# Work lists of a fused convolution and expert kernel, refilled: fewer first singles, more second pairs, and one group's scatters without an index copy

## The chip, the cores and the metric

The kernel runs on one core of a Trainium2 chip. Its time is the device time of one execution in microseconds (us). Before the change the median of three runs is 1198.82 us (1196.96 to 1201.81). A difference of under 0.5% is not told from no change here.

## The reference, cut to what matters

The input `x` is 8 x 2880 x 192, so there are 23040 tokens of 192 numbers. First comes a causal convolution with its own weights at each token: 7 taps for each of 8 heads of 24 numbers, normalised by a softmax.

```
w = exp(weight_gen - max) / sum                 # per token and head, 7 taps
x[s, h, :] = sum_k w[s, h, k] * x_pad[s + k, h, :]
g = argmax(x @ w_group)                         # 4 groups
e = argmax(x @ w_expert[g])                     # 4 experts in the group
out = p_g * p_e * (relu(x @ w1[g, e]) @ w2[g, e])   # 192 -> 1024 -> 192
```

Each token goes to one of 16 experts. All is float32.

## The kernel before, in words

**Two halves that overlap.** The *front* makes tokens ready: convolution, scores, choice of the expert, and a scatter that sends each token's row to its place in a table `rows` in device memory. There each expert has its own stretch (two experts share one from both ends). The *blocks* read runs of rows of one expert from that table, do the two matrix products, and scatter the result to `out`. The 180 columns of 128 tokens are worked in 15 groups of 12 columns (`WIDTHS`). TensorE does the products; VectorE does nearly all of the convolution; ScalarE evacuates and casts; GpSimd issues the scatters; SyncE loads weights and rows.

**Lists.** After certain groups VectorE writes a *list*: which expert's rows the next blocks take. An entry of `ROUNDS` is (groups finished, triples, pairs, singles): a single is a block of 128 rows, a pair of 256, a triple of 384. So the first list, after two groups, has ten singles; the second, after the third group, has four pairs; and so on, 14 lists in all. Before the last list, a slot takes full units of 128 rows only. The last list also has `SHORT` = (7, 4) slots: seven blocks of 320 rows and four of 192, for experts whose last unit is at most half full. How many blocks there are, and of what kind, is fixed when the program is written; which expert each takes is read at run time (SyncE loads an offset and an expert number from the list, L816, L830). What does not fit falls to a tail of conditional blocks (`tail`, L1193).

**Three kinds of arithmetic.** A single is *plain*: full float32 products. Pairs and triples up to the twelfth list are *whole* (`whole`, L1023): w1 and x are split into high and low parts and the first product takes five faster passes, the second product is full float32. From the thirteenth list on (`WHOLE = 12`) w2 is split as well (L870 to L876), and the second product takes the passes of L993 and L994.

**Order of the work.** The order on TensorE, ScalarE, VectorE and SyncE is written out by hand when the program is built. `blocks` (L1035) goes through all blocks unit by unit: it emits the first product (`gemm1`, L940), the second with a lag of two units (`gemm2`, L974), the transposes of the next block (`prep_x`, L910: L926 and L927, for singles L915), and the loads. After every unit `fill` puts in steps of the front until a planned VectorE clock has come up to the planned TensorE clock plus a margin (`AHEAD`). So VectorE's front work is laid beside TensorE's blocks, step by step, by planned costs. A pair also takes VectorE time for the low parts of w1 and x (L861, L936, recorded at the helper's L883); a single takes none.

**From a group to its list.** `ranks` (L440) ends with each token's place (`posi`, L503), then GpSimd scatters 12 columns (L505 to L507), then `table` writes the list. A block's rows may be loaded (L818) only when the scatters of its list's last group have landed. For groups in `SPACED` each scatter first copies its column of row numbers to a ring of three small tiles (L514 to L516), and so a fourth scatter waits until the first has read its numbers; groups outside `SPACED` scatter straight from `posi`:

```
for s in range(n):
    run("pool", 2.2 if g in SPACED else 1.28, clk["dve"])
    scatter_row(pi[:, s:s + 1], xrow[s // SC][:, s % SC, :], round_of(g), g in SPACED)
```

The scatters of results (L1008) stand in the same GpSimd program. At most eight result tiles `y` are in use.

Of the kernel before, what the change touches and what calls it, by code (L numbers as in the profile page):

```python
# [17 lines left out]
DRAM = bass.MemoryType.DRAM  # L18

WIDTHS = (12,) * 15  # L20
ROUNDS = ((2, 0, 0, 10), (3, 0, 4, 0), (4, 0, 5, 0), (5, 0, 7, 0), (6, 0, 5, 0), (7, 0, 7, 0), (8, 0, 5, 0), (9, 0, 6, 0), (10, 0, 7, 0), (11, 0, 5, 0), (12, 1, 4, 0), (13, 0, 5, 0), (14, 0, 6, 0), (15, 3, 2, 2))
SHORT = (7, 4)
LATE = (1.0, 3.0, 3.0)
AHEAD = (1.0, 1.0, 2.5)
HURRY = 12
SPACED = range(2, 15)
HALVES = (36.0, 42.0, 48.0, 54.0, 60.0, 66.0, 72.0, 78.0)
WHOLE = 12
SINGLE = tuple((k,) for k in range(7))
# [13 lines left out]
def conv_moe_kernel(ctx: ExitStack, tc: tile.TileContext, x, wgen, w_group, w_expert, w1, w2, out):  # L43
# [26 lines left out]
    MAXB = NTOK // BK  # L70
    NR = len(ROUNDS)
    ENDS = [r[0] for r in ROUNDS]
    COL = [sum(WIDTHS[:g]) for g in range(len(WIDTHS) + 1)]
# [5 lines left out]
    FIRST = ENDS[0]  # L79
    MAIN = next(r[0] for r in ROUNDS if r[1] or r[2])  # L80
    kinds = ((3, 1), (2, 2), (1, 3))
# [4 lines left out]
    sure = 0  # L86
    for r in ROUNDS[:-1]:
        for nb, c in kinds:
            sure = max(sure, min(sure + nb * UB * r[c], COL[r[0]] * P - NE * (nb * UB - 1)))
    left = (NTOK - sure + NE * (BK - 1)) // BK  # L90
    TAIL = max(0, -(-(left - ROUNDS[-1][2]) // TB))

# [162 lines left out]
    def run(eng, cost, *deps):  # L255
        clk[eng] = max([clk[eng]] + [d + HOP for d in deps]) + cost
        return clk[eng]
# [10 lines left out]
    def round_of(g):  # L268
        return next(r for r in range(NR) if g < ENDS[r])
# [170 lines left out]
    def ranks(g, o, ls, tls):  # L440
# [64 lines left out]
# [3 lines that stand above are left out]
        if g + 1 in ENDS:  # L508
# [3 lines left out]
    def scatter_row(idx, src, r, spaced):  # L512
        ix = idx
        if spaced:  # L514
            ix = new_ix()
            nc.gpsimd.tensor_copy(out=ix, in_=idx)  # L516
        written_once(nc.gpsimd.indirect_dma_start(  # L517
            out=rows[:, :], out_offset=bass.IndirectOffsetOnAxis(ap=ix, axis=0),
            in_=src, in_offset=None, bounds_check=NROW - 1, oob_is_err=False), r)
# [11 lines left out]
    def table(r):  # L531
# [17 lines left out]
        if last:  # L549
# [5 lines left out]
            v.scalar_tensor_tensor(out=at, in0=units, scalar=-3.0, in1=done, op0=ALU.add, op1=ALU.add)  # L555
            for nb, odd, start, slots in ((4, half, at, SHORT[0]), (5, two, None, SHORT[1])):
                cums = yield from listing(r, nb, odd, t, False, start)
# [3 lines left out]
                yield 0.6  # L561
        todo = [(nb, c) for nb, c in ((kinds[0], kinds[2], kinds[1]) if last else kinds) if ROUNDS[r][c] or last and nb == 2]
        for nb, c in todo:
# [32 lines left out]
    def listing(r, nb, n, t, counted, at=None):  # L596
        v = nc.vector
        per = tiles_of(nb)
        at = done if at is None else at
        cume, cums, org = t("cume"), t("cums"), t("org")  # L600
        own, tv, ri = t("own"), t("tv"), t("ri", (P, 2))
        tab = tabs[r, nb] = tb.tile([P, 3], I32, name=f"tab{nb}", bufs=1 if nb in CUT else 4)
        q0 = qp[:, 0:1]
        v.tensor_tensor_scan(out=cume, data0=smask[SG][:, :, 1], data1=n, initial=0.0, op0=ALU.mult, op1=ALU.add)
        v.tensor_tensor(out=cums, in0=cume, in1=n, op=ALU.subtract)
        v.tensor_scalar(out=past[:, 1:], in0=cume, scalar1=q0, scalar2=None, op0=ALU.is_le)
        v.scalar_tensor_tensor(out=org, in0=cums, scalar=float(per), in1=at, op0=ALU.mult, op1=ALU.subtract)
        v.tensor_tensor(out=own, in0=past[:, 0:NE], in1=past[:, 1:], op=ALU.subtract)
        v.scalar_tensor_tensor(out=tv, in0=org, scalar=qb[:, per - 1:per], in1=down, op0=ALU.subtract, op1=ALU.mult)
        v.tensor_reduce(out=ri[:, 1:2], in_=past[:, 1:], axis=AX.X, op=ALU.add)  # L610
        yield 0.9
        v.tensor_tensor(out=tv, in0=tv, in1=first[nb], op=ALU.add)
        v.tensor_scalar(out=tab[:, 1:2], in0=ri[:, 1:2], scalar1=float(NE - 1), scalar2=None, op0=ALU.min)
        v.tensor_tensor(out=tv, in0=tv, in1=own, op=ALU.mult)
        if counted:
            v.tensor_copy(out=tab[:, 2:3], in_=cume[:, NE - 1:NE])
        v.tensor_reduce(out=ri[:, 0:1], in_=tv, axis=AX.X, op=ALU.add)
        v.tensor_scalar(out=tab[:, 0:1], in0=ri[:, 0:1], scalar1=float(NROW), scalar2=None, op0=ALU.add)
        yield 0.9
        return cums  # L620
# [163 lines left out]
    for r, spec in enumerate(ROUNDS):  # L784
        for nb, c in kinds:
            order += [(r, nb, q) for q in range(spec[c])]
            if r == NR - 1:
                order += [(r, k, q) for j, k in enumerate(CUT) if CUT[k] == nb for q in range(SHORT[j])]
    visits = {}
# [442 lines left out]
```

## Time and profile before

| | |
|---|---|
| runs, median (range) | 1198.82 us (1196.96 to 1201.81) |
| the profiled execution | 1198.2 us, span 1196.6 us, granted clock 0.987 |
| TensorE busy | 1125.1 us, 94% |
| VectorE busy | 955.8 us, 80% |
| ScalarE busy | 643.9 us, 54% |
| GpSimd busy | 583.6 us, 49% |
| moved | 275.10 MB, mean 230 GB/s |

A row of the profile names the line of the kernel, the engine (PE is TensorE, DVE VectorE, ACT ScalarE, POOL GpSimd), the operation, the tiles it writes and reads, and its count; in a group row the busy time, the mean duration in ns and the idle time before it follow. In a row of the timeline the start and the duration in us come first, and in brackets the idle time of the engine just before and what ended it.

### The profile page before, as it was taken

How to read it: one execution, taken by the hardware profiler on the slowest of the kernel's cores; microseconds unless marked ns; L12 is line 12 of the kernel's file. 1: busy time of each engine (PE TensorE's matmuls, PEld its weight loads, DVE VectorE, ACT ScalarE, POOL GpSimd, SP SyncE). 2: the span in 40 equal slices, each digit the busy share in tenths (PEclk: the TensorE clock that was granted, in tenths of full speed). 3: DMA queues.
4: the chain of work that ended last, by engine and by line, in shares of the span. 5: the costliest groups of instructions: out<-in, count | busy, mean ns of one | idle time of the engine just before them, and what ended most of it. 6: DMA issues, size and time to landing. Idle time of an engine off the chain costs nothing.

```text
span 1196.6 us, 24607 instructions
## 1 busy us (share of the span) xinstructions
PE 1125.1 (94%) x8357; PEld 1062.7 (89%) x8357; DVE 955.8 (80%) x1682; ACT 643.9 (54%) x1235; POOL 583.6 (49%) x613
## 2 busy tenths in 40 slices
PE   5887999999999999999999999999799899999998
PEld 2444888999999999999989999999699899999997
DVE  8899997989998989998988889898374576655661
ACT  1332435555555555565546556565446676555762
POOL 7164284647274745765564738384636312222211
PEclk9898999999999999999999999999999999999999
DMA  5797999887878877778786868767657875655562
GB/s 172 216 312 227 298 310 286 247 272 229 286 233 255 256 249 235 248 246 281 221 284 197 289 202 281 232 181 227 201 154 235 263 241 154 189 174 179 161 200 76
DMA packets 84521, 275.10 MB, mean 230 GB/s; under 512 B 15491, under 2 KB 34379, under 8 KB 82593
## 3 DMA queue, kind: packets, MB, share of 16 engines
q1 hardware_dynamic: 64056, 229.77, 61.3%
q0 software_dynamic: 20208, 43.39, 11.9%
q8 instruction: 67, 1.10, 0.4%
q14 instruction: 70, 0.57, 0.1%
q10 hardware_dynamic: 120, 0.28, 0.1%
HBM read 225.83 MB, written 48.42 MB: 229 GB/s over the span
## 4 chain that ended last, share of the span: by engine, by line
PE 62%; issue 19%; DVE 6%; POOL 4%; ACT 3%; DMA 3%; another core or an unknown queue 2%; POOLq 1%; SPq 0%; DVEq 0%; ACTq 0%
PE py L991 27%; PE ph L953 25%; POOL out L1008 4%; DVE pr L307 2%; PE pl L389 2%; PE ph L348 1%; PE tpx L927 1%; PE tpx L926 1%; DMA xb<-rows 1%; PE tpx L348 1%; PE tp L406 1%; DMA rows<-rem 1%; PE py L348 1%; PE pl L406 1%
## 5 line engine op out<-in xcount | busy, mean ns | idle before, releaser
L953 PE MATMUL ph<-xh,wa 128*128 128x256 f32 (+3 forms) x1992 | 455.5, 303 | 1.2 <-issue 1.1
L1008 POOL DMA_INDIRECT out<-y,xb x189 | 213.9, 1132 | 425.6 <-ACT y L1000 176.7
L991 PE MATMUL py<-wc,hh 128*128 128x192 f32 x2160 | 401.3, 327 | 2.7 <-ACT y L1000 2.2
L953 PE MATMUL ph<-xl,wa 128*128 128x256 f32 (+3 forms) x1328 | 351.9, 286 | 0.3
L991 PEld LDWEIGHTS py<-wc,hh 128*128 128x128 f32 x2160 | 346.0, 190 | 4.7 <-ACT y L1000 2.8
L953 PEld LDWEIGHTS ph<-xh,wa 128*128 128x128 f32 x1992 | 337.7, 190 | 4.2 <-issue 2.1
L959 ACT ACTIVATE hh<-ph 128x512 f32<-128x512 f32 (+2 forms) x296 | 165.9, 561 | 265.9 <-PE ph L953 239.0
L953 PEld LDWEIGHTS ph<-xl,wa 128*128 128x128 f32 x1328 | 252.1, 190 | 1.1 <-issue 0.8
L307 DVE TENSOR_TENSOR pr<-xin,wt 128x1152 f32<-128x1152 f32 x186 | 249.3, 1351 | 4.7 <-PE py L348 3.4
L517 POOL DMA_INDIRECT rows<-xrow,ix x156 | 222.2, 1424 | 45.6 <-POOL ix L516 31.5
L325 DVE TENSOR_TENSOR xrow<-xrow,pr 128x1152 f32<-128x1152 f32 x144 | 194.9, 1353 | 0.7
L883 DVE SCALAR_TENSOR_TENSOR pr<-ph,hh 128x320 fp32r<-128x320 f32 (+2 forms) x128 | 71.7, 560 | 92.5 <-ACT hh L964 85.6
L883 DVE TENSOR_TENSOR wa<-raw,wa 128x1024 fp32r<-128x1024 f32 x83 | 101.3, 1220 | 31.9 <-ACT wa L859 30.7
L516 POOL COPY ix<-posi 128x1 int32<-128x1 int32 x156 | 76.0, 499 | 79.1 <-DMA rows<-xrow,ix 44.7
L993 PE MATMUL py<-wc,hh 128*128 128x384 f32 x352 | 111.6, 364 | 0.0
L964 ACT ACTIVATE hh<-ph 128x320 fp32r<-128x320 f32 (+2 forms) x128 | 63.8, 499 | 72.0 <-PE ph L953 71.1
L994 PE MATMUL py<-wc,pr 128*128 128x192 f32 x352 | 88.5, 251 | 0.0
L859 ACT CAST wa<-raw 128x1024 fp32r<-128x1024 f32 x83 | 87.1, 1050 | 0.0
L868 ACT CAST wa<-raw 128x1024 fp32r<-128x1024 f32 x83 | 86.8, 1046 | 0.0
L1000 ACT ACTIVATE y<-py,xb 128x192 f32<-128x192 f32 x179 | 67.3, 423 | 20.9 <-PE py L991 16.7
L883 DVE TENSOR_TENSOR xl<-tpx,xh 128x512 fp32r<-128x512 f32 (+1 forms) x92 | 59.3, 644 | 11.4 <-ACT xh L933 10.4
L993 PEld LDWEIGHTS py<-wc,hh 128*128 128x128 f32 x352 | 66.5, 189 | 1.3
(194 smaller groups left out, 1355.4 us busy)
## 6 DMA issues: line engine op xcount, KB each, us to landing
wc<-in_moe_w SPq DMA_DIRECT2D x73, 768.0 KB
raw<-in_moe_w SPq DMA_DIRECT2D x83, 512.0 KB
xin<-in_x SPq DMA_DIRECT2D x14, 1728.0 KB
raw<-in_moe_w SPq DMA_DIRECT2D x91, 256.0 KB
raw<-w1lo SPq DMA_DIRECT2D x83, 256.0 KB
raw<-in_moe_w SPq DMA_DIRECT2D x22, 768.0 KB
xb<-rows SPq DMA_DIRECT2D x75, 194.0 KB
wa<-in_moe_w SPq DMA_DIRECT2D x24, 384.0 KB
```

What stands on the lines that cost most here:

```text
L307: nc.vector.tensor_tensor(out=dst, in0=o.xin[:, c0 + k:c0 + k + SC, :].rearrange("p s (h g) -> p s h g", g=HG), in1=w4[:, c0:c0 + SC, :, k ...
L325: nc.vector.tensor_tensor(out=acc, in0=acc, in1=prs[k - 2], op=ALU.add)
L517: written_once(nc.gpsimd.indirect_dma_start(out=rows[:, :], out_offset=bass.IndirectOffsetOnAxis(ap=ix, axis=0), in_=src, in_offset=None, ...
L859: nc.scalar.copy(out=o.wa[:, 0, :], in_=o.raw[0])
L868: nc.scalar.copy(out=o.wa[:, 2, :], in_=o.raw[1])
L883: f(*a, **k)
L953: nc.tensor.matmul(ph[:, v, :], lhsT=w[:, f0:f0 + P], rhs=rhs, start=i == 0, stop=i == len(terms) - 1)
L959: nc.scalar.activation(out=hh, in_=ph, func=AF.Relu)
L991: nc.tensor.matmul(b.acc[t], lhsT=hh[:, v, c], rhs=wc[0][:, f, :], start=f == 0 and not (b.wide and t == 1), stop=f == NFT - 1 and not (b. ...
L993: nc.tensor.matmul(b.py[t], lhsT=hh[:, v, c], rhs=wc[f // 4][:, f % 4].rearrange("p l d -> p (l d)"), start=f == 0, stop=False)
L994: nc.tensor.matmul(b.acc[t], lhsT=hl[:, v, c], rhs=wc[f // 4][:, f % 4, 0, :], start=False, stop=f == NFT - 1)
L1008: ins = nc.gpsimd.indirect_dma_start(out=out[:, :], out_offset=bass.IndirectOffsetOnAxis(ap=b.x.bitcast(I32)[:, t, D + 1:D + 2], axis=0), ...
```

## The change

The lists hold other numbers of blocks, and the third group (index 2) leaves `SPACED`, which also lowers its planned GpSimd cost from 2.2 to 1.28 us a scatter.

```
-ROUNDS = ((2, 0, 0, 10), (3, 0, 4, 0), (4, 0, 5, 0), (5, 0, 7, 0), (6, 0, 5, 0), (7, 0, 7, 0), (8, 0, 5, 0), (9, 0, 6, 0), (10, 0, 7, 0), (11, 0, 5, 0), (12, 1, 4, 0), (13, 0, 5, 0), (14, 0, 6, 0), (15, 3, 2, 2))
-SHORT = (7, 4)
+ROUNDS = ((2, 0, 0, 8), (3, 0, 5, 0), (4, 0, 5, 0), (5, 0, 7, 0), (6, 0, 5, 0), (7, 0, 6, 0), (8, 0, 6, 0), (9, 0, 6, 0), (10, 0, 6, 0), (11, 0, 6, 0), (12, 1, 3, 0), (13, 1, 4, 0), (14, 0, 6, 0), (15, 0, 6, 2))
+SHORT = (9, 2)
 LATE = (1.0, 3.0, 3.0)
 AHEAD = (1.0, 1.0, 2.5)
 HURRY = 12
-SPACED = range(2, 15)
+SPACED = range(3, 15)
```

In blocks: the first list goes from 10 singles to 8; the whole pairs of lists 2 to 12 from 60 to 59, spread otherwise; the whole triples from 1 to 2; the six pairs of list 13 stay; the last list goes from 3 triples, 7 blocks of 320, 2 pairs, 4 blocks of 192 and 2 singles to no triple, 9 of 320, 6 pairs, 2 of 192 and 2 singles. That is 95 blocks before and 94 after, with room for 23488 rows in both.

## Rows read from the trace of the kernel before

**Rows 1.** The page, part 1: busy time, share of the span, instructions.
```profile
PE 1125.1 (94%) x8357; PEld 1062.7 (89%) x8357; DVE 955.8 (80%) x1682; ACT 643.9 (54%) x1235; POOL 583.6 (49%) x613
```

**Rows 2.** Windows: busy PE, PEld, DVE, ACT, POOL, then clock, DMA share, GB/s.
```profile
160.00:194.00 34.00, 30.09 (x251) 28.36 (x249) 26.48 (x64) 12.22 (x31) 19.24 (x21) 0.95 1.01 314
382.70:440.80 58.10, 56.69 (x454) 55.53 (x453) 53.62 (x85) 33.39 (x62) 33.71 (x34) 1.00 0.80 254
```

**Rows 3.** Timeline of PE: first products that open blocks, whole kinds and singles.
```profile
149.48 0.39 PE L953 MATMUL ph<-xd,wa 96*128 96x128 f32 x2
...
162.28 0.39 PE L953 MATMUL ph<-xd,wa 96*128 96x128 f32 x2
...
315.25 0.41 PE L953 MATMUL ph<-xh,wa 128*128 128x256 f32 x1
...
325.55 0.42 PE L953 MATMUL ph<-xh,wa 128*128 128x256 f32 x1
...
784.46 0.47 PE L953 MATMUL ph<-xh,wa 128*128 128x384 f32 x1
...
802.05 0.36 PE L953 MATMUL ph<-xh,wa 128*128 128x256 f32 x1
```

**Rows 4.** Timeline of PE: first products that open blocks after the twelfth list.
```profile
957.69 0.31 PE L953 MATMUL ph<-xh,wa 128*128 128x256 f32 x1
...
967.34 0.42 PE L953 MATMUL ph<-xh,wa 128*128 128x256 f32 x2
...
1007.23 0.36 PE L953 MATMUL ph<-xh,wa 128*128 128x384 f32 x1
...
1022.01 0.47 PE L953 MATMUL ph<-xh,wa 128*128 128x320 f32 x2
...
1091.87 0.34 PE L953 MATMUL ph<-xh,wa 128*128 128x320 f32 x1
...
1147.58 0.39 PE L953 MATMUL ph<-xh,wa 128*128 128x192 f32 x2
...
1157.01 0.38 PE L953 MATMUL ph<-xh,wa 128*128 128x192 f32 x2
```

**Rows 5.** Timeline of POOL: first and last steps of the second and third group's scatters.
```profile
91.97 1.05 POOL L517 DMA_INDIRECT rows<-xrow,posi  x1 [10.35 <-DVE units L542]
...
107.82 0.97 POOL L517 DMA_INDIRECT rows<-xrow,posi  x1 [0.30 <-issue]
...
142.84 0.31 POOL L516 COPY ix<-posi 128x1 int32<-128x1 int32 x2 [3.27 <-DVE posi L503]
...
172.76 0.98 POOL L517 DMA_INDIRECT rows<-xrow,ix  x1 [0.28 <-POOL ix L516]
```

**Rows 6.** Timeline of PE: its two waits at the end of the singles.
```profile
179.66 0.52 PE L991 MATMUL py<-wc,hh 128*128 128x192 f32 x1 [1.65 <-ACT y L1000]
...
194.35 0.33 PE L926 MATMUL tpx<-ident,xb 128*128 128x128 f32 x1 [1.14 <-DMA xb<-rows]
```

**Rows 7.** The page, part 5: VectorE's low parts of w1 and of x.
```profile
L883 DVE TENSOR_TENSOR wa<-raw,wa 128x1024 fp32r<-128x1024 f32 x83 | 101.3, 1220 | 31.9 <-ACT wa L859 30.7
...
L883 DVE TENSOR_TENSOR xl<-tpx,xh 128x512 fp32r<-128x512 f32 (+1 forms) x92 | 59.3, 644 | 11.4 <-ACT xh L933 10.4
```

**Rows 8.** Timelines, sixth list: last scatter of its group, first use of its rows.
```profile
425.05 1.80 POOL L517 DMA_INDIRECT rows<-xrow,ix  x1 [0.28 <-POOL ix L516]
...
433.27 0.41 ACT L908 COPY xd<-xb 128x256 f32<-128x256 f32 x1 [4.76 <-DMA xb<-rows]
```

**Rows 9.** Timelines, seventh list: the same two steps, the use on PE.
```profile
495.95 0.98 POOL L517 DMA_INDIRECT rows<-xrow,ix  x1 [0.28 <-POOL ix L516]
...
510.97 0.27 PE L926 MATMUL tpx<-ident,xb 128*128 128x128 f32 x1
```

**Rows 10.** Timeline of PE: the longest wait after the first list.
```profile
866.18 0.47 PE L433 MATMUL pl<-ident,xT 128*128 128x128 f32 x1 [6.79 <-ACT xT L425]
```

**Rows 11.** Waits, all engines: who waited for whom, us, times, longest.
```profile
ACT xT L425 <- remote: 27.1, 4, 9.3
```

## The prediction

> **What bounds the kernel now.** I read the page first: TensorE is busy for 1125.1 of 1196.6 us [rows 1], so the question is which blocks it works through and where it waits. Then the windows, list by list. While the fifth list runs, TensorE is busy for 56.7 of 58.1 us and VectorE for 53.6 [rows 2]: TensorE bounds, but VectorE, which makes the rows, has only 8% to spare. Then the timeline of TensorE, to get a price per block from the starts of neighbouring blocks. A single costs (162.28 - 149.48) / 2 = 6.4 us, a whole pair 10.3, a whole triple at most 17.6 [rows 3]. After the twelfth list a pair costs 9.65, a triple 14.8, a block of 320 rows (1091.87 - 1022.01) / 5 = 14.0, a block of 192 rows 9.4 [rows 4]. Last come the waits of TensorE, few and named below.
>
> **Part 1, the lists: what TensorE has to do.** The blocks are fixed in number, so their sum is a count times a price.
> - Two singles less: -2 x 6.4 = -12.8.
> - One whole pair less: -10.3.
> - One whole triple more. The only one in the trace took 17.6 with some of the front's transposes between its products, so that is the upper bound; the triple with split w2 took 14.8 [rows 4]. For two tiles the whole kind costs 10.3 - 9.65 = 0.65 more than the split kind, so for three tiles about 1.0 more: 14.8 + 1.0 = 15.8, which I take (an estimate).
> - Last list: three triples less, -44.4; two blocks of 320 more, +28.0; four pairs more, +38.6; two blocks of 192 less, -18.8. Together +3.4.
>
> The sum is -12.8 - 10.3 + 15.8 + 3.4 = -3.9 us, with the triple's bounds -4.9 to -2.1. None of it lies beside other work: TensorE sets the end. Every block's loads, casts and scatters go with it, and DMA traffic falls with the two singles, which move 1.57 MB of weights in 6.4 us each.
>
> Both sets of lists must be full for that count. I counted the tokens of the reference's routing for its own inputs (1194 to 1852 per expert) through the rules of the lists: every slot is used before and after, and the last list's six pair slots meet six pairs, so the conditional tail stays empty as it does now.
>
> **Part 2, the third group's scatters.** Twelve copies leave GpSimd, and so does the ring of three. The group's scatters ran from 142.84 to 173.74; the second group's, which have no copies, took from 91.97 to 108.79, that is 16.8 us instead of 30.9 [rows 5]. So the second list's rows come some 14 us earlier, at about 160 plus the landing. That is what the list needs: with two singles less its first pair is due 12.8 us earlier. Between the end of the rows' path and the first pair's transposes nothing is then late in the new order.
>
> The cost side: the twelve scatters go out in a burst while single blocks fetch weights, and in the stretch just behind it the DMA engines are already full (share 1.01 at 314 GB/s) [rows 2]. The scatters move the same bytes, only sooner, and each single's weights are asked for about two blocks (12.8 us) ahead; that covers it. Without the cover, half the bandwidth for 17 us would delay the weights by at most 17 x (1 - 157/246) = 6 us, with 157 as half of 314 and 246 as 1.57 MB in 6.4 us. I take 0. This is a rival below. The Trainium skill (DMA: Bandwidth & Descriptors, section on queues, rings and completion order) says that a DMA engine takes turns between the queues that have work for it; by that rule a queue of many scatters takes turns with the weights for as long as it has work, which speaks against the burst. No row here shows the turns themselves.
>
> GpSimd also gets to the result scatters sooner. Now they stand behind the third group's, and at the end of the singles TensorE waits 1.65 us for a result's evacuation and 1.14 for the second list's first rows [rows 6], and over those 34 us the granted clock is 0.95: 1.7 us are lost at the lower of its two levels, 1.2 GHz, after the first of these waits [rows 2]. All gone: -4.5. All back, because the weights of pairs, the next group's input and the scatters still meet there: 0. I take half, -2.2.
>
> **Part 3, what is late next: the rows of lists 6 and 7.** The front's steps are laid beside TensorE's blocks, so I compare how much earlier each list is asked for with how much earlier its rows come.
> - TensorE reaches lists 3 to 6 with two singles less and one pair more: 12.8 - 10.3 = 2.5 us earlier. It reaches list 7 a further pair earlier (list 6 has six pairs, not seven): 12.8 us.
> - VectorE goes the other way. A pair takes 1.22 + 0.64 = 1.9 us of it [rows 7], a single none, and 12.8 us of singles make room for 1.24 pairs: the front is 2.4 us later at the same point of TensorE's work.
> - What room is there? Rows of list 6: last scatter issued at 426.85, first use held up for them until 433.27, with a wait of 4.76 us on ScalarE [rows 8]: room 0, and 6.4 us from scatter to use. Rows of list 7: 496.93 + 6.4 = 503.3, used at 510.97 [rows 9]: room 7.6.
> - So list 6 comes late by 2.5 + 2.4 = 4.9 us and list 7 by 12.8 + 2.4 - 7.6 = 7.6. If VectorE goes on while TensorE waits, the first wait counts toward the second, and 7.6 is the sum; if its queue stands behind the waiting block's low part of x, the two add up to 12.5. Lower bound 0, if the new order on paper happens to bring the steps of the front forward. I take 7.6.
>
> **Part 4, one wait in the last group's routing.** At 866.18 TensorE has waited 6.79 us for ScalarE with no block's product between the two steps [rows 10]. ScalarE's wait there is one of four such, 27.1 us in all [rows 11], among 13 groups routed after the start; the other three had products beside them. What releases it the profile does not name, so I treat it as a lot: kept with 4 in 13, gone with 9 in 13, -4.7. Bounds -6.8 and +6.8 (a second one exposed).
>
> **The sum.** -3.9 - 2.2 + 7.6 - 4.7 = -3.2 us. The profiled execution took 1198.2 us (1.6 outside the span), 0.6 under the median of the runs, so the forecast is 1195.0.
>
> **Rivals.**
> - *The rows come in time.* Part 3 costs nothing: VectorE has idle time, and a front that is emitted earlier in the pairs uses it. For it: VectorE's 4.5 idle us in 58 [rows 2]. Against it: list 6 has no room already [rows 8]. -3.9 - 4.5 - 4.7 = -13.1: 1185.1.
> - *Slower: waits for rows in full.* The place is the first transposes of lists 6 and 7. It decides when VectorE's front falls behind TensorE by more than the room there, and when its queue is held with TensorE: +12.5, and nothing comes back at the singles or in the last group: -3.9 + 12.5 = +8.6: 1206.8. For it: the rooms of 0 and 7.6 us [rows 8, 9]. Against it: VectorE's idle time lets it catch up a little in each group.
> - *The burst delays weights.* 6 us in the singles on top of the forecast: 1201.0. For it: the full DMA engines [rows 2]. Against it: two blocks of lead.
> - *The change does not do what it says.* If the lists leave one more pair than my count, a round of three conditional pairs runs with nothing laid beside it, at least 3 x 9.65 = 29 us: about 1224. Against it: the count leaves no expert's last unit within a token of the limits.
>
> **How the numbers follow.** Forecast 0.43, rows in time 0.26, waits in full 0.20, burst 0.08, tail 0.03. The forecast's own range is 1189 to 1201. Within 0.5% (about what a measurement of this kernel can tell from no change) is 1192.8 to 1204.8. Of the forecast a third lies below that, 0.15, and 0.28 inside; rows in time is faster, 0.26; waits in full is slower except a small part, 0.18 and 0.02; the burst is inside, 0.06, or slower, 0.02; the tail slower. Faster 0.41, same 0.36, slower 0.23. To leave out no more than 2 in 10 the range runs from 1183 to 1208.
>
> **What would show each step.** Part 1: the starts of neighbouring blocks at the same prices, 94 blocks, and the last list starting some 7 us earlier relative to the waits before it and taking 3.4 us more. Part 2: the third group's twelve scatters within 17 to 20 us and straight from `posi`, and the first pair's transposes with no wait for rows. Part 3: ScalarE's copies `xd` waiting for `xb` at the first pairs of lists 6 and 7, with an idle TensorE behind them. Part 4: no idle stretch of several us before L433 in the last group. The prediction is wrong if the first pairs of lists 6 and 7 start without a wait, or if TensorE's busy time does not fall.

## The result and the profile after

The change made the kernel slower: 1215.1 us (1208.97 to 1218.87, six runs) against 1196.7 (1191.44 to 1201.81, six runs), ratio 1.0145 with a 95% interval of 1.0116 to 1.0173. That is outside the range of 1183 to 1208. The profiled execution took 1208.97 us, its span is 1207.3, 10.7 over the one of before. It is the fastest of the six, so its trace accounts for 10.7 of the 18.4 us between the medians.

One thing has to be known for all that follows. In four of the six comparisons of this study the kernel before took 1197 to 1203 us, in the other two (the sets e5 to e8 and e9 to e12) 1176 and 1173 us. I call them the first and the second kind. The expectations say "a chip like the first" and "like the second"; a chip of the same number turned up once in either kind, so whether it is the chip or what else runs beside it stays open. The traces of the two kinds differ plainly in one point, waits of ScalarE that are shown below, and half of the result hangs on it.

The page, part 1, of the changed kernel, answers to [rows 1]. TensorE is busy for nearly the same time in a longer span: 1124.2 against 1125.1 us.

```profile
PE 1124.2 (93%) x8333; PEld 1063.0 (88%) x8333; DVE 959.8 (79%) x1687; ACT 646.8 (54%) x1235; POOL 568.0 (47%) x601
```

The blocks' prices are those of before, as the openers of a block of 320 rows and of a pair show (TensorE's timeline, answers to [rows 4]): 13.97 and 9.66 us.

```profile
1012.77 0.34 PE L953 MATMUL ph<-xh,wa 128*128 128x320 f32 x1
...
1026.74 0.34 PE L953 MATMUL ph<-xh,wa 128*128 128x320 f32 x1
...
1138.58 0.31 PE L953 MATMUL ph<-xh,wa 128*128 128x256 f32 x1
...
1148.24 0.42 PE L953 MATMUL ph<-xh,wa 128*128 128x256 f32 x2
```

Where the time goes is seen from the times at which TensorE opens a list, read from the same view:

| opens | before | after | after - before | by the blocks alone |
|---|---|---|---|---|
| list 2 | 199.0 | 190.7 | -8.3 | -12.8 |
| list 3 | 247.2 | 251.1 | +3.9 | -2.5 |
| list 4 | 303.0 | 308.0 | +5.0 | -2.5 |
| list 6 | 440.8 | 446.1 | +5.3 | -2.5 |
| list 7 | 518.1 | 516.5 | -1.6 | -12.8 |
| list 11 | 784.5 | 790.7 | +6.2 | -2.5 |
| list 13 | 913.2 | 912.9 | -0.3 | -7.3 |
| list 14 | 977.2 | 984.1 | +6.9 | -7.3 |
| end of the span | 1196.6 | 1207.3 | +10.7 | -3.9 |

(The last column counts blocks at the prices of the prediction.) 4.5 us are lost up to the second list and 2 more up to the third; between lists 11 and 13 the change is 1.7 better than its blocks, and in list 13 it loses 7.2.

So the waits have to be found. From 130 us on the timeline of TensorE has these of over 2 us, and one of 1.54 (in brackets the idle time just before, and what ended it); the first two answer to [rows 6], the sixth to [rows 10]. One more like the fifth and sixth, at 759.76, is 1.91 us.

```profile
149.50 0.33 PE L407 MATMUL tp<-ident,rem 128*128 128x128 f32 x1 [2.38 <-ACT rem L399]
160.96 0.69 PE L991 MATMUL py<-wc,hh 128*128 128x192 f32 x1 [4.44 <-issue]
239.58 0.33 PE L926 MATMUL tpx<-ident,xb 128*128 128x128 f32 x1 [1.54 <-DMA xb<-rows]
300.41 0.33 PE L926 MATMUL tpx<-ident,xb 128*128 128x128 f32 x1 [2.21 <-DMA xb<-rows]
503.18 0.33 PE L433 MATMUL pl<-ident,xT 128*128 128x128 f32 x1 [3.55 <-ACT xT L425]
879.19 0.47 PE L433 MATMUL pl<-ident,xT 128*128 128x128 f32 x1 [4.57 <-ACT xT L425]
945.53 0.48 PE L926 MATMUL tpx<-ident,xb 128*128 128x128 f32 x1 [9.20 <-DMA xb<-rows]
```

By the table two places carry most: the singles (149 and 161) and the thirteenth list (945).

**The singles.** The twelve scatters ran as forecast, without copies, in 16 us (GpSimd's timeline, answers to [rows 5]):

```profile
142.19 0.97 POOL L517 DMA_INDIRECT rows<-xrow,posi  x1 [3.48 <-DVE units L542]
...
157.27 0.97 POOL L517 DMA_INDIRECT rows<-xrow,posi  x1 [0.30 <-issue]
```

Just there ScalarE's steps that take over a product of TensorE wait, and the profile can name nothing that ended the wait ("remote"); its timeline:

```profile
148.66 0.38 ACT L959 ACTIVATE hh<-ph 128x256 f32<-128x256 f32 x1 [1.83 <-remote]
...
158.35 0.37 ACT L917 COPY xd<-tp 96x256 f32<-96x256 f32 x1 [1.69 <-remote]
160.49 0.42 ACT L1000 ACTIVATE y<-py,xb 128x192 f32<-128x192 f32 x1 [1.77 <-remote]
162.76 0.38 ACT L959 ACTIVATE hh<-ph 128x256 f32<-128x256 f32 x1 [1.85 <-remote]
```

The windows (columns as in [rows 2]; the first is of the kernel before, the rest of the changed one, and the last answers to the first of [rows 2]) show what it costs: TensorE is busy for 11.0 of 17 us instead of 16.5, then the granted clock is 0.80, and the DMA engines are less busy than before, not more (0.86 against 0.89, and 0.89 against 1.01).

```profile
143.00:160.00 17.00, 16.53 (x131) 16.03 (x130) 16.69 (x31) 7.22 (x19) 14.58 (x15) 1.00 0.89 266
```

```profile
143.00:160.00 17.00, 11.03 (x73) 10.21 (x71) 16.80 (x28) 4.78 (x12) 12.85 (x13) 0.90 0.86 286
160.00:177.00 17.00, 16.04 (x102) 16.04 (x103) 5.82 (x7) 6.30 (x15) 2.21 (x3) 0.80 0.75 221
160.00:194.00 34.00, 31.27 (x255) 30.27 (x256) 19.24 (x31) 16.36 (x37) 4.70 (x4) 0.90 0.89 277
```

The delay is handed on. The first pair's w1 is asked for in good time (at 152.31 on SyncE's queue), but ScalarE's cast of it stands in ScalarE's own order behind the steps of singles that TensorE now does late. It starts at 173.97, right behind one of them, and VectorE, which had gone ahead, stands 11 us in its own queue behind that cast (its timeline):

```profile
175.04 1.23 DVE L883 TENSOR_TENSOR wa<-raw,wa 128x1024 fp32r<-128x1024 f32 x1 [11.18 <-ACT wa L859]
```

Group 4's row numbers then come at 201.20 us; in the kernel before they came at 189.24 (VectorE's timeline, first of after, then of before):

```profile
201.20 0.17 DVE L503 SCALAR_TENSOR_TENSOR posi<-pos 128x12 int32<-128x12 f32 x1
```
```profile
189.24 0.17 DVE L503 SCALAR_TENSOR_TENSOR posi<-pos 128x12 int32<-128x12 f32 x1
```

Behind that, lists 3 and 4 wait for rows (239.58 and 300.41). The stalls are not needed for these two waits: e9 below has them without a stall, with 1.65 and 2.18 us, and there VectorE stands 9.58 us behind the first pair's transposes, which wait for rows.

**The thirteenth list.** Its third pair took 22.2 us; the same pair took 15.1 in the kernel before, and an undisturbed one takes 9.65. TensorE waits there for the rows of the fourth pair, whose transposes stand between the third pair's products. These rows are loaded only at 943.12 (SyncE), after the last padding (L589) and results of earlier blocks behind it (L1008) on GpSimd:

```profile
937.32 0.67 POOL L589 DMA_DIRECT2D rows<-rem  x1 [0.77 <-issue]
938.29 1.04 POOL L1008 DMA_INDIRECT out<-y,xb  x1 [0.31 <-issue]
```
```profile
943.12 0.34 SPq L818 DMA_DIRECT2D xb<-rows  x1
```
Before that SyncE had waited 14.6 us for a scatter of results to land (its view of waits from 912 to 960 us); in the kernel before it has no such wait in this list:
```profile
SPq L818 <- DMA out<-y,xb: 14.6, 1, 14.6
```

The load needs the buffer of a block whose result is still to be scattered. There is room for twelve row tiles in all; a pair takes two, a triple three. With the second triple in list 12 the buffer was last used five blocks ago, in the kernel before six (`place`, L218).

### The profile page after: what moved, and what is told of

It reads as the page before. It is cut to its first block, busy times and chain, and to the rows that moved or that the text cites. A ratio compares the mean times of both kernels' runs of the same rounds, so it can differ in the third digit from the quotient of the medians.

```text
span 1207.3 us, 24517 instructions
## 1 busy us (share of the span) xinstructions
PE 1124.2 (93%) x8333; PEld 1063.0 (88%) x8333; DVE 959.8 (79%) x1687; ACT 646.8 (54%) x1235; POOL 568.0 (47%) x601
## 4 chain that ended last, share of the span: by engine, by line
PE 75%; DVE 7%; issue 6%; DMA 3%; ACT 3%; POOL 2%; another core or an unknown queue 2%; POOLq 1%; SPq 0%; ACTq 0%; DVEq 0%
PE ph L953 32%; PE py L991 26%; PE py L993 4%; DVE pr L307 3%; PE py L994 2%; PE tpx L926 2%; PE tpx L927 2%; PE pl L389 1%; PE pl L993 1%; PE ph L348 1%; PE tp L406 1%; DMA raw<-in_moe_w 1%; DMA raw<-w1lo 1%; DVE pr L343 1%
## 5 line engine op out<-in xcount | busy, mean ns | idle before, releaser
L953 PE MATMUL ph<-xh,wa 128*128 128x256 f32 (+3 forms) x2016 | 460.4, 303 | 0.9 <-issue 0.8
L1008 POOL DMA_INDIRECT out<-y,xb x189 | 207.5, 1098 | 452.3 <-ACT y L1000 204.1
L953 PEld LDWEIGHTS ph<-xh,wa 128*128 128x128 f32 x2016 | 341.6, 190 | 5.7 <-issue 3.9
L953 PEld LDWEIGHTS ph<-xl,wa 128*128 128x128 f32 x1344 | 255.3, 190 | 0.9 <-issue 0.7
L517 POOL DMA_INDIRECT rows<-xrow,ix x144 | 207.5, 1441 | 45.2 <-POOL ix L516 28.6
L993 PE MATMUL py<-wc,hh 128*128 128x384 f32 x368 | 117.2, 366 | 0.0
L516 POOL COPY ix<-posi 128x1 int32<-128x1 int32 x144 | 70.0, 496 | 72.3 <-DVE posi L503 37.5
L994 PE MATMUL py<-wc,pr 128*128 128x192 f32 x368 | 92.9, 252 | 0.1
```

Source lines behind the costliest of these rows:

```text
L517: written_once(nc.gpsimd.indirect_dma_start(out=rows[:, :], out_offset=bass.IndirectOffsetOnAxis(ap=ix, axis=0), in_=src, in_offset=None, ...
L953: nc.tensor.matmul(ph[:, v, :], lhsT=w[:, f0:f0 + P], rhs=rhs, start=i == 0, stop=i == len(terms) - 1)
L993: nc.tensor.matmul(b.py[t], lhsT=hh[:, v, c], rhs=wc[f // 4][:, f % 4].rearrange("p l d -> p (l d)"), start=f == 0, stop=False)
L994: nc.tensor.matmul(b.acc[t], lhsT=hl[:, v, c], rhs=wc[f // 4][:, f % 4, 0, :], start=False, stop=f == NFT - 1)
L1008: ins = nc.gpsimd.indirect_dma_start(out=out[:, :], out_offset=bass.IndirectOffsetOnAxis(ap=b.x.bitcast(I32)[:, t, D + 1:D + 2], axis=0), ...
```

## The experiments

All ratios are to the kernel before, run beside.

**e1: the copy-free scatters alone** (first kind). In the kernel before:
```
-SPACED = range(2, 15)
+SPACED = range(3, 15)
```


> The kernel before with one part of the change alone: the third group's twelve scatters take their row numbers without a copy, lists as before. Theory A (the unspaced scatters fall into the singles and cost there): the twelve scatters run in about 16 us instead of 30, TensorE loses 5 us or more among the singles that run beside them, group 4's row numbers come later than 189 us, and the time is 1202 to 1207 us against 1197. Theory B (the scatters cost nothing, the lists are the loss): the first pair's rows come 14 us earlier than they are needed, the two waits of 1.65 and 1.14 us at the end of the singles go, and the time is 1193 to 1197 us.


Measured: 1213.23 us, ratio 1.0065 (1.0038 to 1.0091), some 8 us. TensorE has both stalls among the singles, with the lists of before:
```profile
152.21 0.48 PE L407 MATMUL tp<-ident,rem 128*128 128x128 f32 x1 [3.27 <-ACT rem L399]
...
164.04 0.69 PE L991 MATMUL py<-wc,hh 128*128 128x192 f32 x1 [3.71 <-ACT y L1000]
```
Theory A held; group 4's numbers came at 198.7. Not all of the loss in this trace lies at the burst: TensorE opens list 2 at 208.9 (199.0 in the kernel before) and list 5 at 398.3 (382.7). Between the two it waits 3.93 us at 383.06 beside another run of scatters, and the kernel before does not. How much such later waits add to the 8 us was not measured.

**e2: the lists alone** (first kind): the changed kernel with `SPACED = range(2, 15)`.


> The changed kernel with the third group's scatters spaced by copies again, its lists as changed. Theory A: the loss among the singles (TensorE idle 2.4 and 4.4 us there, and its half clock) goes, group 4's row numbers come near 190 us instead of 201, and 5 to 8 us of the 18 us come back: 1207 to 1210 us; the first pair of the second list may wait some us for its rows. Theory B: the loss stays, 1213 to 1217 us, or grows by a wait of up to 9 us for the first pair's rows. Theory C (a second loss, at list 13) says of both that TensorE still waits about 9 us there for the rows of its pair.


Measured: 1212.12 us, ratio 1.0067 (1.0034 to 1.0099). No stall in the burst's place, as theory A said, but the wait for the first pair's rows, and that of list 13, are there:
```profile
185.01 0.48 PE L926 MATMUL tpx<-ident,xb 128*128 128x128 f32 x1 [6.81 <-DMA xb<-rows]
...
947.42 0.47 PE L926 MATMUL tpx<-ident,xb 128*128 128x128 f32 x1 [10.11 <-DMA xb<-rows]
```
The two halves, 0.65 and 0.67%, come near to the whole of 1.45%.

**e3: one triple** (first kind). In the changed kernel:
```
-(13, 1, 4, 0), (14, 0, 6, 0), (15, 0, 6, 2))   SHORT = (9, 2)
+(13, 0, 5, 0), (14, 0, 6, 0), (15, 0, 6, 3))   SHORT = (9, 2)
```


> The changed kernel with list 12 as five pairs (no whole triple) and the last list refilled to suit (three singles, nine short triples, two short pairs). By the block durations this is 6.6 us more TensorE work than in the changed kernel. Theory C (the extra triple takes three of the twelve row slots, so that a pair of list 13 takes over a slot that was last used five blocks before instead of six, by blocks whose results stand behind the last group's scatters and the padding): the wait of 9.2 us in list 13 falls to about 2, as in the kernel before, with its half clock, and the time stays at 1213 to 1217 us in spite of the added work. Rival: the wait comes from list 13's rows being made late by anything else; it stays near 9 us and the time is 1220 to 1223 us.


Measured: 1217.03 us, ratio 1.0104 (1.0060 to 1.0148). The wait fell from 9.20 to 3.06 us, so theory C held. By the prediction's prices the edit adds 0.9 us of work (one single more, +6.4, and a triple turned into a pair, -5.5), not the 6.6 of the expectation. The changed kernel had 1.0145 in its own comparison; that e3's 1.0104 is less fits the shorter wait, but the two intervals overlap.
```profile
949.77 0.33 PE L926 MATMUL tpx<-ident,xb 128*128 128x128 f32 x1 [3.06 <-DMA xb<-rows]
```

**e4, and e14 once more: the later lists alone** (first kind both). The kernel before's first two lists and spacing, the changed kernel's lists from the sixth, last list `(15, 0, 9, 2)` with `SHORT = (7, 2)`, that is nine pairs, two singles, seven blocks of 320 and two of 192 rows; the list in e4's expectation is garbled.


> The kernel before's first two lists (ten singles, four pairs) and its spaced scatters, with the changed kernel's lists from list 6 on; the last list has nine short... seven short triples, two short pairs and nine singles in two blocks' place so that everything fits; by block durations 1 us more than the changed kernel and 4.3 us more than the kernel before. Theory A with C: nothing is lost among the singles or in lists 3 and 4, only the wait in list 13 (about 7 us more than before) and the 4.3 us: 1206 to 1210 us. If the early lists and scatters cost nothing, the time is that of the changed kernel, 1215 us.

> The kernel before's first two lists and spaced scatters, the changed kernel's lists from list 6 on, with the extra triple; last list of nine pairs, two singles, seven short triples, two short pairs. By block durations 0.4 us more than the kernel before up to list 13's end less 4.9, last list 4.8 more: about the same sum. Theory C: TensorE waits 7 to 8 us in list 13 against 3.5, with half clock, and the time is 0.2 to 0.6% over the kernel before. Rival: the wait comes with the early lists; then it is near 3.5 us here and the time is within 0.2%.


Measured: 1200.82 us, ratio 0.9970 (0.9939 to 1.0000), and 1198.89 us, ratio 0.9997 (0.9963 to 1.0031). List 13 waits 7.30 and 6.18 us, so that wait belongs to the triple and not to the early lists, but the time is not the 1206 to 1210 us that e4 expected, beside 1203.25 for the kernel before in this set. One reason is its count: the 4.3 us more of work are those of the last list alone and leave out the two pairs less and the triple more of the lists before, and e14's "about the same sum" is right. In e4's trace the long wait of [rows 10] is 0.63 us, which gives about the same amount back; e16 shows what such waits go with.
```profile
935.42 0.48 PE L926 MATMUL tpx<-ident,xb 128*128 128x128 f32 x1 [7.30 <-DMA xb<-rows]
```

**e5: bursts among the pairs** (second kind). In the kernel before `SPACED = (2, 3, 4, 9, 10, 11, 12, 13, 14)`.


> The kernel before, where groups 6 to 9 (numbers 5 to 8) scatter their rows without copies, in the stretch of the pairs, while the third group keeps its copies. Theory A1 (unspaced scatters cost wherever they run): each of the four bursts stalls TensorE by some us, together 8 us or more, 1205 us and over against 1197. Theory A2 (they cost only among the singles, where the weights of a single come in every 6.4 us): the rows of these groups come earlier, TensorE idles no more than before in the stretch from 330 to 600 us, and the time is the kernel before's within 3 us.


Measured: 1174.13 us, ratio 0.9978 (0.9959 to 0.9996). No stall of TensorE in the four bursts: by this set A2 stood. For the first kind it was the wrong conclusion, as e16 shows.

**e6: twelve buffers for the third group's row numbers** (second kind):
```
+iys = [iy[:, k:k + 1] for k in range(SG)]
-ix = new_ix()
+ix = iys.pop(0) if r == 1 else new_ix()
```


> The kernel before, with the copies of the third group's row numbers kept but in twelve columns of their own instead of three in turn: a copy no longer has to wait until an earlier scatter has read its numbers. Theory A3 (what protects the singles is the limit of three scatters under way): the twelve scatters run in about 16 to 20 us as without copies, and the loss is that of the copy-free kernel, 1202 to 1208 us. Rival A4 (it is POOL's time that the copies take): the scatters stay 2.0 us apart or more, the singles are as in the kernel before, 1195 to 1199 us.


Measured: 1172.99 us, ratio 0.9971 (0.9957 to 0.9985). The copies ran first and the scatters 1.28 us apart, so it is the three buffers that space them and not the copies' time. No stall, against A3.

**e7, e12: one set of weights for the singles** (second kind both). e1 with
```
+if part and 0 < n < ROUNDS[0][3]:
+    o.wa, o.wc = visits[0].wa, visits[0].wc
+    return
```


> The kernel before with the third group's copy-free scatters, where the second to tenth single multiply by the first single's weights and load none of their own (their results differ; the loads of nine singles, 1.5 MB each, are left out). Theory A2 (the burst costs by meeting the singles' weights in the DMA engines): TensorE's idle time between 140 and 180 us falls under 2 us and its clock stays at its upper level there. Rival A1 (the burst by itself delays TensorE's signals to ScalarE): the two stalls of about 3 us and the half clock are there as in the copy-free kernel, while DMA is nearly idle.

> The copy-free kernel where the second to tenth single multiply by the first single's weights and load none (their results differ), once more, for a chip like the first: if the stalls need the singles' weight traffic beside the burst, TensorE idles under 2 us between 140 and 180 us there; if the burst alone makes them, the two stalls of about 3 us are there. On a chip like the second nothing is told apart: no stall in either.


Measured: 1170.21 and 1170.06 us, one run each. No stall, but none is there with the weights either (e10), so nothing is told apart.

**e8: no burst, no second triple** (second kind): e4 with list 12 of five pairs, last list `(15, 0, 7, 2)`, `SHORT = (8, 3)`.


> The kernel before's first two lists and spaced scatters, the changed kernel's lists from list 6 on, list 12 as five pairs (one whole triple in all), last list of seven pairs, two singles, eight short triples, three short pairs. By block durations 2.5 us under the kernel before. If the burst, the shorter singles and the extra triple are the whole loss, none of it is left and the time is 1192 to 1197 us; if the later lists cost by themselves it is 1200 or more.


Measured: 1177.14 us, ratio 1.0008 (0.9989 to 1.0028): nothing of the loss is left.

**e9, e10, e11: the changed kernel, e1 and e2 again** (second kind).


> The changed kernel as it is, beside experiments of the same chip. The runs so far were on two chips: on the first the kernel before took 1197 to 1203 us and TensorE's signals to ScalarE came some us late in places, on the second it took 1176 us and none of those waits was there. Theory A (the 18 us are the burst's late signals, the lists' early end and the row slots): on a chip like the first the loss is 1.2 to 1.6% again; on one like the second only the row slots are left, with the longer last list, 0.2 to 0.7%. Theory B (the lists lose by their amount of work alone): 1.4% on any chip.

> The kernel before with the third group's scatters copy-free, once more. Theory A: on a chip like the first again 0.4 to 0.9% slower with two stalls of TensorE among the singles; on one like the second no stall there and a time within 0.3% of the kernel before, or up to 0.3% less, as with the twelve row numbers. If the loss is there on any chip without the stalls, the cause is another.

> The changed kernel's lists with the third group's scatters spaced, once more. The first pair's rows are asked for too early on any chip: a wait of 5 to 8 us with half clock at the end of the singles, and about 9 us at list 13 for the row slots. So 0.6 to 1.0% slower than the kernel before on any chip; if the list 13 wait is due to late signals, it is gone on a chip like the second and the loss is under 0.5%.


Measured: 1183.74 us, ratio 1.0102 (1.0079 to 1.0125); 1173.35, 1.0004 (0.9987 to 1.0022); 1183.97, 1.0093 (1.0071 to 1.0115). The burst costs nothing here, the lists 0.9%. For the changed kernel that is more than theory A's 0.2 to 0.7%, which had left out the wait for the first pair's rows, and less than theory B's 1.4%. In the changed kernel the last of the third group's scatters goes out at 157.9, the pair's rows are loaded at 166.25, behind 1728 KB of another group's tokens, and TensorE has them at 183.69. Its timeline, then SyncE's, then the windows of e9 and, last, of e10:
```profile
183.69 0.47 PE L926 MATMUL tpx<-ident,xb 128*128 128x128 f32 x1 [6.36 <-DMA xb<-rows]
...
920.72 0.48 PE L926 MATMUL tpx<-ident,xb 128*128 128x128 f32 x1 [7.97 <-DMA xb<-rows]
```
```profile
165.07 0.34 SPq L134 DMA_DIRECT2D xin<-in_x  x1
166.25 0.34 SPq L818 DMA_DIRECT2D xb<-rows  x1
```
```profile
160.00:184.00 24.00, 14.87 (x147) 13.37 (x145) 14.88 (x19) 8.10 (x19) 9.16 (x4) 0.93 1.03 323
```
```profile
160.00:184.00 24.00, 22.30 (x207) 20.91 (x205) 20.87 (x39) 9.89 (x26) 10.98 (x5) 1.00 1.02 323
```
In both the DMA engines are full at 323 GB/s. Two singles more keep TensorE busy in that stretch. With two singles less it opens list 2 10.6 us earlier (189.6 in e9, 200.2 in e10) and not 12.8, and list 3 3.6 us later (251.3 against 247.7) and not 2.5 earlier, so 6.1 us of the gain are gone by then.

**e13: the pair's rows ahead of the tokens** (first kind). One swap on SyncE's queue in the changed kernel: `load_group` of group 5 a little later, `n == (4 if g == 4 else ...)`.


> The changed kernel, with one swap on SP's queue: the first pair's rows are loaded before a group's weights of the convolution and tokens (1.73 MB) instead of just behind them. Theory D (the DMA engines are full there, and the pair's 0.2 MB wait behind the 1.73 MB and the weights): on a chip like the second the 6.4 us wait before the pair's transposes falls under 2 us, with its half clock, and 3 to 6 us of the 12 us come back; group 4's row numbers come some us earlier too or stay. Rival D1 (the rows are complete only late): the wait stays 5 us or more and the time stays at 1.0% over the kernel before.


Measured: 1214.9 us, ratio 1.0119 (1.0068 to 1.0170). In this kind the stalls of the burst (3.34 and 4.10 us) come first and hide the wait for rows in the changed kernel too, so it says nothing on theory D.

**e15, e16: bursts again, on the first kind.** e16 is e5 and e6 together; e15 adds a later token load.


> The kernel before with its own lists and three edits: twelve columns for the third group's row numbers (copies kept), copy-free scatters in groups 6 to 9, and the token load of the window moved behind a single's and a pair's weights on SP's queue. If theory D holds, the wait of 3 us of the last single for its row falls, and the three gains add: 0.4 to 0.8% faster than the kernel before on a chip like the second; on one like the first the burst costs 0.5% and the sum is near none. If the token load comes too late for the convolution of its group, VectorE waits for it and the time is no better than 0.3%.

> The kernel before with the first two of these edits alone (twelve columns, copy-free scatters in groups 6 to 9). If the gains add: 0.4 to 0.6% faster on a chip like the second. If both came from the same slack: 0.2 to 0.3%.


Measured: 1257.03 us, ratio 1.0474 (1.0423 to 1.0525), and 1255.89, 1.0463 (1.0414 to 1.0512): 56 us, where the same edits one by one gained 0.2 and 0.3% on the second kind, and where e15 had expected near nothing on this kind. e16 has five bursts, and TensorE waits 5.51, 9.98, 7.85, 9.93 and 4.91 us beside them. GpSimd's first and last scatter of one burst in e16, ScalarE's two steps around it, and TensorE's last product that the second of them needs:
```profile
341.10 1.12 POOL L519 DMA_INDIRECT rows<-xrow,posi  x1 [0.30 <-issue]
...
355.30 0.97 POOL L519 DMA_INDIRECT rows<-xrow,posi  x1 [0.31 <-issue]
```
```profile
342.97 0.60 ACT L961 ACTIVATE hh<-ph 128x512 f32<-128x512 f32 x1 [2.94 <-PE ph L955]
357.95 0.60 ACT L961 ACTIVATE hh<-ph 128x512 f32<-128x512 f32 x1 [14.38 <-remote]
```
```profile
343.94 0.28 PE L955 MATMUL ph<-xl,wa 128*128 128x256 f32 x1
...
358.90 0.47 PE L929 MATMUL tpx<-ident,xd 128*128 128x128 f32 x1 [9.98 <-ACT xd L910]
```
By the profile the product is over at 344.2, and TensorE starts others until 348.65; ScalarE goes on at 357.95, 1.7 us after the last scatter of the burst is issued. The Trainium skill (Perfetto Trace Analysis, section Tensor Engine Instruction) says that a product's end in the profile is estimated from its size, and that its semaphore goes out only when PSUM has acknowledged the writes. The trace agrees in that the delay lies behind the end shown. Since that end is an estimate, the trace does not tell whether the product itself or only its signal was late. The same stretch of 20 us in e16 and, below it, in e5:
```profile
340.00:360.00 20.00, 8.57 (x56) 7.87 (x55) 6.41 (x22) 2.67 (x6) 12.62 (x13) 0.79 0.52 162
```
```profile
340.00:360.00 20.00, 20.00 (x154) 19.87 (x153) 19.59 (x17) 13.18 (x26) 11.61 (x11) 1.00 0.92 301
```

The waits of [rows 10] and [rows 11] in the kernel before can be read the same way. ScalarE's 9.3 us there run from 856.4 to 865.65, and the run of rows' and results' scatters that GpSimd issues beside it ends at 864.4 (the kernel before, the run's last three on GpSimd, then ScalarE):
```profile
860.89 0.97 POOL L517 DMA_INDIRECT rows<-xrow,ix  x1 [0.30 <-issue]
862.16 0.97 POOL L1008 DMA_INDIRECT out<-y,xb  x1 [0.30 <-issue]
863.44 0.97 POOL L1008 DMA_INDIRECT out<-y,xb  x1 [0.30 <-issue]
```
```profile
865.65 0.48 ACT L425 COPY xT<-pl 128x384 f32<-128x384 f32 x1 [9.27 <-remote]
```
Every profile of the first kind but that of e17 has such "remote" waits of ScalarE (34 us in the kernel before, 88 in e16, by the view of waits); no profile of the second kind has one. All those of over 4 us lie beside a run of at least four scatters with no more than 0.6 us between them; most end within 2.5 us of the run's last scatter, some while it still goes on.

**e17: results spaced too** (first kind). In the kernel before:
```
+to = new_ix()
+nc.gpsimd.tensor_copy(out=to, in_=b.x.bitcast(I32)[:, t, D + 1:D + 2])
-... IndirectOffsetOnAxis(ap=b.x.bitcast(I32)[:, t, D + 1:D + 2], axis=0)
+... IndirectOffsetOnAxis(ap=to, axis=0)
```


> The kernel before, with each scatter of results given a copy of its row numbers too, from the same three buffers in turn as the rows' scatters: no two scatters of POOL run back to back any more. Theory A1 (POOL's back-to-back scatters hold up TensorE's signals to ScalarE): on a chip like the first the waits of ScalarE for late signals (27 us for xT at line 425) fall under 8 us, the wait of 6.8 us in list 12's stretch goes, and the time is 0.4 to 1.5% less; on one like the second, where no signal is late, the time is within 0.3%. Rival: the late signals there have another cause; they stay, and the copies change nothing or cost by holding result slots longer (0 to 0.5% slower).


Measured: 1252.65 us, ratio 1.0470 (1.0436 to 1.0505). Half of theory A1 held: no wait named "remote" is left. The time went the other way, which neither expected. With one ring of three buffers for rows and results GpSimd waits for scatters to land (247.7 us before the new copies alone), and the rows come late; the row of the copies in part 5 of the page, ScalarE's view of waits and one of TensorE's nine waits of over 2 us for a pair's rows:
```profile
L1009 POOL COPY ix<-xb 128x1 int32<-128x1 int32 x189 | 63.8, 345 | 272.3 <-DMA out<-y,ix 247.7
```
```profile
ACT xd L908 <- DMA xb<-rows: 79.2, 13, 15.6
```
```profile
466.25 0.47 PE L926 MATMUL tpx<-ident,xb 128*128 128x128 f32 x1 [12.15 <-DMA xb<-rows]
```

**e18: the changed kernel with one set of weights** (first kind), the edit of e7.


> The changed kernel where the second to eighth single multiply by the first single's weights and load none (their results differ). On a chip like the first: if the burst needs the weight traffic, TensorE idles under 2 us between 140 and 175 us; if the burst alone holds the signals, two stalls of 2 to 5 us with half clock are there. On one like the second, theory D (the first pair's rows wait in full DMA engines) expects that the wait of 6.4 us before the pair's transposes is under 1 us; rival D1 (they are complete late), that it stays over 4 us.


Measured: 1216.0 us, one run. The two stalls are there, with the DMA engines at 0.06 until the burst begins at 148.08. So the singles' weights are not needed for them. The second question has no answer on this kind.
```profile
140.00:150.00 10.00, 10.00 (x79) 9.80 (x79) 9.45 (x37) 4.27 (x11) 2.62 (x3) 1.00 0.06 20
```
```profile
156.43 0.47 PE L407 MATMUL tp<-ident,rem 128*128 128x128 f32 x1 [3.43 <-issue]
168.24 0.43 PE L994 MATMUL py<-wc,hh 128*128 128x192 f32 x1 [3.36 <-ACT y L1003]
```

No version is known to beat the kernel before in both kinds: e6 is 0.3% faster in the second, and its edit is part of what loses 4.6% in the first.

## Why the prediction was wrong

**The step that failed** is the cost side of Part 2: "I take 0", with 6 us of late weights as the only price. The burst cost about 8 us by itself (e1) on the first kind, and not through the weights: ScalarE learned of TensorE's products late while GpSimd issued scatters back to back. The bound was drawn around the DMA engines because the burst's bytes were the only thing I weighed. The rival *the burst delays weights* had the place and nearly the size, with a wrong mechanism (e18) and a chance of 0.08. That the scatters and the weights share the DMA engines, which the prediction held against the burst, was not what decided: in the stalls the engines were at 0.52 to 0.86, not full. The lists lost as much again (e2: 0.67%), by the two omissions below. On the second kind, where the burst costs nothing, they make the changed kernel 1.0% slower by themselves.

**Part 2, the gain.** The scatters took 16 us as said, and the last of them went out 15 us earlier than before (157.27 against 172.76). But "nothing is then late in the new order" left out the load of these rows. Of the 34 us that I had read with the DMA share at 1.01 [rows 2], the pair's 0.2 MB had to find their way through the same engines. On the second kind this wait is 6.36 us with copy-free scatters and 9.69 with spaced ones (e9, e11). On the first it is hidden in the changed kernel, since TensorE has lost as much in the burst. Whether the tokens ahead of the load make the wait was not settled (e13 fell on the kind where it does not show).

**Part 1.** The counts and prices held: 94 blocks, 14.0 us for 320 rows, 9.65 for a pair, the last list 3.8 us longer (predicted 3.4). The two triples took 16.9 and 16.8 us with some of the front's work between their products, inside the bounds. What the sum of work left out is that a triple also takes three of twelve row tiles, so that a later load waits for results to be scattered. That is a wait of 9.2 us in list 13 against 2.1 and 1.3 in the kernel before, and e3, by taking one triple away, brought it to 3.06.

**Part 3.** Rows were late, but not where I put them. List 7 had no wait, which the prediction had named as a sign of being wrong: its rows were used at 510 as before. TensorE opened it only 1.6 us earlier than in the kernel before, and not 12.8, since it had lost the rest on the way; so the 7.6 us of room were never used up, and whether VectorE would have kept up was not tested. At list 6 ScalarE waited 4.21 us, as in the kernel before (4.76) [rows 8], and TensorE under 1. Lists 3 and 4 lost 1.5 and 2.2 us instead, after VectorE had been held for 11 us behind the cast of the first pair's w1. So 7.6 us were forecast and about 4 came, by another road.

**Part 4.** I treated the long wait as a lot, kept with 4 in 13, since the profile does not name its releaser. It recurred with 4.57 us, and two more like it came in other groups (3.55 at 503.18, 1.91 at 759.76). These waits go together with runs of scatters on GpSimd, and e17, where copies stand between the scatters, has none. What falls together with such a run differs with the order of the whole kernel: the wait is 0.63 us in e4 and 7.24 in e16. That the next kernel would keep it in 4 cases of 13 was a guess without a mechanism.

## What to carry to other kernels

A spacing or a copy that looks like overhead on an idle engine may go with another engine's signals being on time; before it is removed, look for waits without a named releaser and lay that engine's timeline beside them. When work is taken out ahead of a stage, ask whether the stage's inputs pass through something that is already full, and when a block grows, count the buffers that it takes as well as its time. A result under one set of conditions can reverse under another: e5 and e6 gained 0.2 and 0.3% in one kind, and the two edits together (e16) lost 4.6% in the other.

## What the runs showed of the hardware that was not expected

While GpSimd issues indirect scatters 1.28 us apart, a product of TensorE can become known to ScalarE up to 14 us after the end that the profile shows, and mostly not until 0.5 to 2.5 us after the last scatter (1.7 in e16, 1.2 in the kernel before). In e16 VectorE went on beside it until it needed ScalarE's result. It happens with the DMA engines far from full (0.52). Not every run of scatters does it: beside the second group's twelve [rows 5] no profile has such a wait. With the rows' scatters limited to three under way there is less of it (34 us in the kernel before, 88 in e16), and with a copy before every scatter of results too, in the one run that tried it (e17), there was none. It was so in four comparisons and in no trace of the two others, where three of the same kernels ran (e9, e10, e11). What makes the two kinds is open, and so is the path on which the signal is held.
